# Wq's first half loaded in two pieces: 16 rows, then 112 rows

## The chip, the cores and the metric

The kernel runs on one core of a Trainium2 chip. The metric is device time in microseconds (us), lower is better; three runs of the kernel before gave 198.17, 198.26 and 198.59, with 198.26 as the median. All else comes from one profiled execution, which took 198.21.

## The reference

One decoding step of an attention layer with a gate beside it, for a batch of 8 tokens of width 512. All tensors are bf16.

```
xn = layernorm(x)                                    # 8 x 512
q  = xn @ wq                                         # wq 512 x 4096: 32 heads of 128
k, v = the last 2048 positions of the caches         # 8 batches x 8 kv heads x 2048 x 128 each
s  = softmax(q k^T * 128^-0.5) v @ wo                # 4 query heads share a kv head
g  = silu((sigmoid(xn @ w_gate) * (xn @ w_up)) @ w_down)   # inner width 1792
out = x + s * g
```

The work is small beside the data: the two cache windows are 32 MB each (33.6 million bytes), Wq and Wo 4 MB each, and the three weights of the gate 1.75 MB each.

## The kernel before

All large inputs are loaded by DMA on SP's queue, in tiles of 128 rows (partitions), through one pool of nine buffers (`RING`, the tag "ring"). A tile is 2 MB for Wq's halves, K, V and Wo's halves, and 1.75 MB for the gate's weights. In a K, V or Wq tile each partition holds one run of 16 KB. The function `load` (L88) issues a transfer on SP unless it is told otherwise.

The order of the loads is written out by hand (`loads`, L138 to L146): Wq's two halves, then K and V tiles in turn, where V tile i comes `PV_LAG` steps after K tile i, then the gate's weights and Wo in parts of falling size. A loop (`issue_loads`, L164) issues a load when its buffer has been released by the work on an earlier tile; the framework puts the semaphore waits before it. The completion semaphores of these loads are eight that are used in turn, so a load also waits for the one eight places before it on the hardware queues. The tiny x is loaded once on ACT's queue (`x_bf`, L97, 8 rows of 1 KB) and once on GpSimd's (L184).

Wq is 512 rows of 4096. Row 4p + kt lies on partition p (`wq_view`, L99), so that each partition has four rows of 8 KB; the first half (`wq_sb0`) takes rows kt = 0 and 1, the second kt = 2 and 3. Both stand in memory with a pitch of 32 KB from partition to partition. Their transfers (L104) are the first two that SP issues.

Then the layernorm runs on DVE and ACT (L200 to L228), and `q_projection` (L357) multiplies: 16 matmuls on the first half, 16 on the second (L367). `q_out` (L378) copies and turns q into the block layout `qz_sb` that the scores need. After it a loop of slots runs K's turns on DVE (`k_turn`, L422), the scores on TensorE (`qk`, L435), softmax (L447 to L512), and the product with V (`pv`, L549), each a few slots behind the one before. The gate's matmuls are near the end, and Wo's (L662) last, followed by two DVE instructions and the store of the result.

Of the kernel before, what the change touches and what calls it, by code (L numbers as in the profile page):

```python
# [10 lines left out]
def kernel(  # L11
# [14 lines left out]
    P = 128  # L26
# [32 lines left out]
    CB = CH // C4  # L59
    PV_WIDE = 6  # L60
    RING = 9
    NCOL = 2
    DC = D // NCOL

# [10 lines left out]
    small = ctx.enter_context(tc.tile_pool(name="small", bufs=2))  # L75
    ring = ctx.enter_context(tc.tile_pool(name="ring", bufs=RING))
    ppool = ctx.enter_context(tc.tile_pool(name="ppool", bufs=2))
# [10 lines left out]
    def load(dst, src, q=None):  # L88
        if q is None:
            q = nc.sync  # L90
        q.dma_start(out=dst, in_=src)

    def ring_tile(shape, name):
        return ring.tile(shape, bf16, name=name, tag="ring", align_bytes=ALIGN)
# [4 lines left out]
    wq_view = A_wq.rearrange("(p kt) n -> p kt n", kt=KT)  # L99
    KH = KT // 2  # L100
    wq_sb = []
    for kh in range(2):
        t = ring_tile([P, KH, Hq * Dh], f"wq_sb{kh}")
        load(t[:], wq_view[:, kh * KH : (kh + 1) * KH, :])  # L104
        wq_sb.append(t)

    k_tiles = {}
# [56 lines left out]
    def issue_loads():  # L164
        while loads_done[0] < len(loads):
            n = loads_done[0]
            if n >= RING and loads[n - RING] not in released:
                break
            kind, i = loads[n]
            if kind == 0:  # L170
                k_tiles[i] = load_kv(A_k_cache, i, "k_sb")
            elif kind == 1:
                v_tiles[i] = load_kv(A_v_cache, i, "v_sb")
            elif kind == 2:
                load_mlp(i)
            else:
                load_wo(i)
            loads_done[0] += 1

    issue_loads()  # L180
    x2_sb = work.tile([NCOL * 32, DC], bf16, name="x2_sb")
    nc.gpsimd.memset(x2_sb[:], 0.0)
    for j in range(NCOL):
        nc.gpsimd.dma_start(  # L184
# [124 lines left out]
    hT_sb = work.tile([P, FT, 32], bf16, name="hT_sb")  # L309
    gate = work.tile([NCOL * 32, DC], f32, name="gate")  # L310

# [26 lines left out]
    def unit_out():  # L338
        b_ps = psum1.tile([NCOL * 32, DC], f32, name="b_ps", tag="misc")
        for t in range(FT):  # L340
            for j in range(NCOL):
                nc.tensor.matmul(
                    b_ps[32 * j : 32 * (j + 1), :],
                    lhsT=hT_sb[:, t, :],
                    rhs=wd_sb[0][:, t, DC * j : DC * (j + 1)],
                    start=(t == 0),
                    stop=(t == FT - 1),
                    tile_position=(0, 32 * j),
                    skip_group_check=True,
                )  # L350
        sigb = work.tile([NCOL * 32, DC], f32, name="sigb")
        nc.scalar.activation(out=sigb[:], in_=b_ps[:], func=AF.Sigmoid)
        nc.vector.tensor_tensor(out=gate[:], in0=sigb[:], in1=b_ps[:], op=ALU.mult)
# [357 lines left out]
```

## Time and profile before

| what | value |
|---|---|
| median of three runs | 198.26 us |
| the profiled execution: its time, its span | 198.21 us, 196.5 us |
| DMA: moved, mean rate | 81.19 MB, 413 GB/s |
| SP's queue: packets, share of 16 engines' span | 6752, 97.1% |
| Wq's two issues on SP | 407 and 421 ns |
| Wq, from issue to landing | 7.6 and 11.8 us |
| first q matmul; first of the second half | 8.49 us; 13.16 us |
| last part of Wo landed | 192.96 us |

The span runs from the first to the last instruction of the program; the device's time includes 1.71 us around it. In the table of 40 slices a digit is the busy share of a slice in tenths. DMA stands for the mean of the core's 16 DMA engines. The chain of waits is followed back from the last instruction, at each step to what released it; a stretch of the chain that is called DMA runs from the issue of a transfer to its landing, so it contains the time in which it was queued behind others. Beside these views the trace has a record of every DMA packet: its start, its duration and its bytes. A row of 16 KB is one packet.

### The profile page before, as it was taken

How to read it: one execution, taken by the hardware profiler on the slowest of the kernel's cores; microseconds unless marked ns; L12 is line 12 of the kernel's file. 1: busy time of each engine (PE TensorE's matmuls, PEld its weight loads, DVE VectorE, ACT ScalarE, POOL GpSimd, SP SyncE). 2: the span in 40 equal slices, each digit the busy share in tenths (PEclk: the TensorE clock that was granted, in tenths of full speed). 3: DMA queues.
4: the chain of work that ended last, by engine and by line, in shares of the span. 5: the costliest groups of instructions: out<-in, count | busy, mean ns of one | idle time of the engine just before them, and what ended most of it. 6: DMA issues, size and time to landing. Idle time of an engine off the chain costs nothing.

```text
span 196.5 us, 2699 instructions
## 1 busy us (share of the span) xinstructions
PE 138.2 (70%) x1112; PEld 57.6 (29%) x1112; DVE 117.0 (60%) x200; ACT 32.6 (17%) x68; POOL 9.3 (5%) x21
## 2 busy tenths in 40 slices
PE   0340078669998987899789278946794779674783
PEld 0110011032324222423333044404240424443661
DVE  3818999746686828664777277837773750361101
ACT  3008540410121102101210021002100210340000
POOL 8820000000000000000000000000000000000000
PEclk9999999955999997879999957996888587996579
DMA  6999999999999999999999999999999999999991
GB/s 215 429 427 427 430 434 429 440 434 427 434 427 434 427 427 427 430 434 430 430 434 434 424 427 440 430 425 427 430 434 430 427 431 434 423 424 420 411 391 41
DMA packets 6860, 81.19 MB, mean 413 GB/s; under 512 B 792, under 2 KB 1088, under 8 KB 2112
## 3 DMA queue, kind: packets, MB, share of 16 engines
q1 hardware_dynamic: 6752, 81.01, 97.1%
q8 instruction: 8, 0.13, 0.2%
q10 hardware_dynamic: 32, 0.01, 0.1%
q14 instruction: 4, 0.03, 0.0%
q0 software_dynamic: 64, 0.01, 0.0%
HBM read 81.02 MB, written 0.01 MB: 412 GB/s over the span
## 4 chain that ended last, share of the span: by engine, by line
DMA 72%; DVE 17%; PE 8%; ACT 1%; issue 1%; SPq 0%; DVEq 0%; ACTq 0%
DMA k_sb<-in_A_k_cache_dram 47%; DMA wd_sb<-in_B_w_down_dram 14%; DVE k_sb L422 11%; DMA wq_sb<-in_A_wq_dram 6%; DMA wo_sb<-in_A_wo_dram 5%; PE pT_ps L486 3%; PE s_ps L435 3%; DVE qz_sb L395 2%; PE acc_ps L549 1%; DVE mx L447 1%; DVE qT_sb L386 1%; DVE pt_bf L475 1%; ACT L461 1%; PE q_ps L367 1%; PE mb_ps L456 0%
## 5 line engine op out<-in xcount | busy, mean ns | idle before, releaser
L422 DVE STREAM_TRANSPOSE k_sb<-k_sb 128x1024 f32<-128x1024 f32 x64 | 75.9, 1219 | 16.6 <-DMA k_sb<-in_A_k_cache_dram 16.5
L435 PE MATMUL s_ps<-k_sb,qz_sb 128*32 128x512 bf16 x256 | 68.7, 1065 | 16.4 <-DVE k_sb L422 11.6
L549 PE MATMUL acc_ps<-v_sb,pT_sb 128*32 128x256 bf16 (+1 forms) x416 | 35.3, 345 | 3.9 <-DMA v_sb<-in_A_v_cache_dram 2.6
L549 PEld LDWEIGHTS <-pT_sb 128*32 128x32 bf16 (+1 forms) x416 | 12.5, 109 | 33.2 <-issue 27.0
L506 DVE TENSOR_SCALAR pT_sb<-pc_bf,Hm 128x512 bf16<-128x512 bf16 x32 | 9.1, 349 | 18.3 <-ACT pc_bf L495 18.3
L435 PEld LDWEIGHTS <-qz_sb 128*32 128x32 bf16 x256 | 8.3, 100 | 34.0 <-issue 26.1
L560 ACT COPY acc_sb<-acc_ps 128x256 f32<-128x256 f32 (+1 forms) x16 | 7.2, 453 | 63.2 <-PE acc_ps L549 63.2
L486 PE MATMUL pT_ps<-pt_bf,spread 128*128 128x128 bf16 x128 | 12.5, 272 | 6.3 <-DVE pt_bf L475 6.3
L570 PEld LDWEIGHTS oT_ps<-Sel,acc_sb 128*128 128x128 f32 x88 | 11.8, 202 | 14.3 <-ACT acc_sb L560 8.5
L570 PE MATMUL oT_ps<-Sel,acc_sb 128*128 128x16 f32 x88 | 13.4, 276 | 1.1 <-ACT acc_sb L560 1.1
L486 PEld LDWEIGHTS <-spread 128*128 128x128 bf16 x128 | 10.8, 123 | 10.8 <-DVE pt_bf L475 10.8
L456 PE MATMUL mb_ps<-mj,SumM 128*128 128x4 f32 x16 | 3.5, 286 | 14.3 <-DVE mj L449 14.3
L461 ACT ACTIVATE p_bf<-s_ps,nm 128x512 bf16<-128x512 f32 x8 | 5.5, 687 | 46.5 <-DVE nm L458 46.5
L577 DVE TENSOR_TENSOR oT_sb<-oT_ps,rden 128x16 bf16<-128x16 f32 x16 | 2.6, 160 | 11.7 <-PE oT_ps L570 11.7
L456 PEld LDWEIGHTS mb_ps<-mj,SumM 128*128 128x128 f32 x16 | 2.8, 218 | 22.5 <-DVE mj L449 20.6
L397 ACT COPY qz_sb<-qT_sb 32x128 bf16<-32x128 bf16 x20 | 8.3, 413 | 3.0 <-DVE qT_sb L386 2.7
L530 DVE RECIPROCAL rden<-den_ps 128x32 f32<-128x32 f32 x8 | 2.8, 351 | 7.3 <-PE den_ps L528 7.3
L495 ACT CAST pc_bf<-pT_ps 128x512 bf16<-128x512 f32 x8 | 4.7, 587 | 13.1 <-PE pT_ps L486 13.1
L367 PE MATMUL q_ps<-wq_sb,xnT_sb 128*32 128x512 bf16 x32 | 3.8, 625 | 4.0 <-DMA wq_sb<-in_A_wq_dram 4.0
L475 DVE STREAM_TRANSPOSE pt_bf<-p_bf 128x512 bf16<-128x512 bf16 x8 | 5.4, 679 | 1.9 <-ACT p_bf L461 1.9
L662 PE MATMUL a_ps<-wo_sb,o_sb 128*32 128x256 bf16 x64 | 5.5, 315 | 1.0 <-DMA wo_sb<-in_A_wo_dram 0.9
L447 DVE TENSOR_REDUCE mx<-s_ps 128x1 f32<-128x512 f32 x8 | 5.3, 657 | 0.0
(61 smaller groups left out, 61.9 us busy)
## 6 DMA issues: line engine op xcount, KB each, us to landing
k_sb<-in_A_k_cache_dram SPq DMA_DIRECT2D x16, 2048.0 KB, 31.8
v_sb<-in_A_v_cache_dram SPq DMA_DIRECT2D x16, 2048.0 KB, 29.5
wq_sb<-in_A_wq_dram SPq DMA_DIRECT2D x2, 2048.0 KB, 9.7
wo_sb<-in_A_wo_dram SPq DMA_DIRECT2D x2, 1024.0 KB
wg_sb<-in_B_w_gate_dram SPq DMA_DIRECT2D x1, 1792.0 KB, 29.3
wu_sb<-in_B_w_up_dram SPq DMA_DIRECT2D x1, 1792.0 KB, 30.1
wd_sb<-in_B_w_down_dram SPq DMA_DIRECT2D x1, 1792.0 KB, 27.6
wo_sb<-in_A_wo_dram SPq DMA_DIRECT2D x3, 512.0 KB, 23.5
```

Of the source, the lines that this page charges most:

```text
L397: nc.scalar.copy(out=out, in_=in_)
L422: nc.vector.transpose(out=kw, in_=kw)
L435: nc.tensor.matmul(s_tiles[b][32 * gl : 32 * (gl + 1), :], lhsT=qz_sb[:, b, GL * gg + gl, j, :], rhs=kT[:, :, a, :, gl, e], start=(gg == 0 ...
L447: nc.vector.reduce_max(out=mx[:], in_=s_tiles[b][:], axis=AX.X)
L456: nc.tensor.matmul(mb_ps[:], lhsT=SumM[:], rhs=mj[:], start=True, stop=True)
L461: nc.scalar.activation(out=p_bf[:], in_=s_tiles.pop(b)[:], func=AF.Exp, bias=nm[:], scale=scale, accum_out=den128[:],)
L475: nc.vector.transpose(out=pt_bf[:].rearrange("p c g q r -> p (c g q r)"), in_=p_bf[:])
L486: nc.tensor.matmul(pT_ps[:, :, c4, :], lhsT=spread[:, c4, Q, :], rhs=pt[:, :, Q, :], start=(Q == 0), stop=(Q == NQ - 1), skip_group_check= ...
L506: nc.vector.tensor_scalar(out=pT_tiles[b][:, :, gl, :], in0=pc, scalar1=Hm[:, gl : gl + 1], scalar2=None, op0=ALU.mult,)
L549: nc.tensor.matmul(acc_tiles[i][w * c : w * (c + 1), :], lhsT=pT[:, 32 * y : 32 * y + w], rhs=v_tiles[i][:, ch : ch + n_ch, :].rearrange(" ...
L560: nc.scalar.copy(out=acc_sb[:], in_=acc_tiles.pop(i)[:])
L570: nc.tensor.matmul(oT_ps[:], lhsT=acc_sb[:, Dh * c : Dh * (c + 1)], rhs=sel[:, c // 2, c % 2], start=(c == 0), stop=(c == n_ch - 1),)
```

## The change

The first half of Wq is no longer loaded by one transfer of 128 rows. Two transfers fill the same tile: the first brings partitions 0 to 15, one run of 16 KB for each of the 16 DMA engines, and the second partitions 16 to 127. The second half stays one transfer, and so do all other loads. SP issues one DMA more (47 in place of 46); no other engine's instructions change, apart from the semaphores on which they wait.

```diff
     RING = 9
+    HEAD = 16
...
     for kh in range(2):
         t = ring_tile([P, KH, Hq * Dh], f"wq_sb{kh}")
-        load(t[:], wq_view[:, kh * KH : (kh + 1) * KH, :])
+        rows = (0, HEAD, P) if kh == 0 else (0, P)
+        for r0, r1 in zip(rows, rows[1:]):
+            load(t[r0:r1], wq_view[r0:r1, kh * KH : (kh + 1) * KH, :])
         wq_sb.append(t)
```

## The prediction

> **What bounds the kernel now.** I read the page's first two parts first: is any engine full, or are the transfers?
>
> ```profile
> span 196.5 us, 2699 instructions
> ...
> PE 138.2 (70%) x1112; PEld 57.6 (29%) x1112; DVE 117.0 (60%) x200; ACT 32.6 (17%) x68; POOL 9.3 (5%) x21
> ...
> DMA  6999999999999999999999999999999999999991
> ```
>
> No compute engine is above 70%, while the DMA row stands at 9 in every slice but the first and the last. So the end of the kernel is the start of the transfers, plus 81 MB at a fixed pace, plus a short tail. The chain of waits at both ends says the same: Wq's transfers hold the first 13 us, and from 155 us the chain goes through the loads of w_down and Wo to four short instructions.
>
> ```profile
> 1.29 11.84 DMA wq_sb<-in_A_wq_dram
> 13.16 1.07 PE q_ps L367 x8
> ...
> 155.44 27.61 DMA wd_sb<-in_B_w_down_dram
> ...
> 183.06 9.89 DMA wo_sb<-in_A_wo_dram
> ```
>
> Between these the chain runs for a while through DVE (k_sb, L422), but the DMA engines never run dry: loads are issued about 30 us before they land (DMA issues: k_sb 31.8, v_sb 29.5), about six 2 MB tiles ahead. If Wq comes later, q, the K turns, the released buffers and the next issues all come later by the same amount, and the queue keeps its depth. So a delay or gain in the first transfer reaches the end one for one. The table of stretches shows the start up close (us, then busy times, and last the clock, the DMA share and GB/s):
>
> ```profile
> 0.00:1.75 1.75, 0.00 (x0) 0.00 (x0) 0.00 (x0) 0.31 (x1) 0.85 (x6) 1.00 0.00 0
> 1.75:2.25 0.50, 0.00 (x0) 0.00 (x0) 0.00 (x0) 0.50 (x1) 0.50 (x2) 1.00 1.75 344
> 2.25:3.25 1.00, 0.00 (x0) 0.00 (x0) 0.60 (x2) 0.47 (x1) 0.93 (x4) 1.00 0.57 180
> 3.25:8.25 5.00, 0.29 (x4) 0.31 (x5) 4.22 (x11) 0.29 (x1) 4.74 (x5) 1.00 0.99 418
> ...
> 43.25:183.25 140.00, 111.75 (x918) 46.19 (x919) 83.93 (x144) 18.53 (x39) 0.00 (x0) 0.85 1.01 429
> ```
>
> Nothing moves before 1.75 us, the pace is poor until 3.25, and then it is within 3% of the 429 GB/s of the middle. In the trace's records of single packets (start and duration of each) the poor stretch is this: each of the 16 DMA engines begins its first 16 KB row of Wq between 1.855 and 2.755 us (mean 2.20), that row takes 632 to 1438 ns (mean 1128), and all 16 first rows end between 2.99 and 3.50 (mean 3.32). From then on a row takes 611 ns, on every engine, nearly back to back. That is the whole room for a gain: an unhindered row would save at most 1128 - 611 = 0.52 us, and a start of all engines at the first one's 1.855 another 0.34.
>
> **The change, part by part.**
>
> *One more issue on SP.* The two Wq issues take 407 and 421 ns, so every later one of the first burst moves by 0.41 us: the first K load's issue goes from 1.74 to 2.15, and its bytes are wanted only after Wq, at about 13. Covered by 10 us: 0. Without that cover it would cost 0.41.
>
> *Waits that move.* The loads use eight completion semaphores in turn, so each load waits for the eighth before it. With one more in the row, the sixth K or V load, issued at 5.20 us behind x's long landed semaphore, will wait for the 16-row piece (here at about 4.5), and the next for the 112 rows as it did for the first half; further ones keep their old partners. Queued behind it on SP are loads whose bytes are needed 30 us later: 0. PE's first q matmul (8.49) now waits for two transfers; behind it stand the 31 other q matmuls. The 112 rows are issued last and land last, so the wait for the 16 adds nothing, and PE idles 2.77 us before the second half anyway: 0.
>
> *Sixteen more completion packets* of 4 bytes, one for each engine, 9 ns and some 6 ns of gap: +0.015 us.
>
> *The start of the first rows.* The only small transfer on such a queue is x_bf (8 rows, L97): issued at 0.81 like Wq, its packets start between 1.779 and 1.853, where Wq's spread over 0.9 us. With 16 rows I expect the same close start, at about 1.83 for all engines, 0.37 before today's mean. The 112 rows, issued 0.42 later, are ready at about 2.6 (today's 2.20 and 0.42), before any first row is through.
>
> *The first rows themselves.* Today each engine's first row is one of the eight that it takes of 128, and after 3.5 us these run at 611 ns on all 16 engines at once, so there they do not hinder each other. The new head sends them to 16 neighbouring partitions. No transfer of before does that at this size. From below: the unhindered 611 ns. From above: all 16 in turn, 16 x 0.611 = 9.8 us. The nearest row is again x_bf, 8 neighbouring partitions: its eight packets take 51, 44, 293, 44, 461, 260, 44 and 44 ns, 1241 together, 3.5 times eight unhindered ones. Some of that may be the first read's latency, which the Wq rows have too. I take 3.5 x 0.611 = 2.15 us, and the 0.52 us of first latency ahead of it as today: 1.83 + 0.52 + 2.15 = 4.50, against 3.32. **Term: +1.2 us**; ends -0.9 (0.52 + 0.37) and +8.9 (1.83 + 0.52 + 9.8 - 3.32).
>
> Here the Trainium skill has a price: SBUF — State Buffer, section "Door 1: The DMA port swizzle (why [64,N] ≈ [32,N])", says that partitions 0 to 15 reach 4 of 16 ports and measured 104 GB/s. By it the 256 KB would take 2.5 us in place of my 2.15, and the term would be +1.6. No run shown here moves such a piece.
>
> *The other 112 rows.* Spread over the 16 engines as evenly as the 128 are now (eight packets each), they are 7 per engine, so the borders between engines no longer fall where those of 128 rows do, and two engines come to write into one neighbourhood at once for part of the time. From below: 0, the 611 ns of the 128-row transfers, which are the nearest in size; from above, 3.5-fold on all 7 rows as in x_bf, 7 x 2.5 x 0.611 = +10.7. But a stretch of eight neighbours, which in x_bf has eight engines in it, has only two at 7 rows each: two by turns throughout would cost 7 x 0.611 = 4.3. I take half the time shared: **+2.1 us**. The engines run their own lists without waiting for each other, and the end is set by the last one, so I do not lower this for those that meet nobody.
>
> **The sum**, on the profiled execution: its span is 196.5 and its time 198.21, 0.05 below the median of 198.26. 198.21 + 1.2 + 2.1 + 0.015 = **201.5 us**, 1.6% slower.
>
> **Rivals.**
>
> 1. *Only the 16 rows are hindered*; the 112 are laid out as harmlessly as 128. For it: every 128-row transfer runs at 611 ns. Time 198.21 + 1.2 = **199.4**. Chance 0.18.
>
> 2. *The 112 rows go out by turns*, one row to each engine, so that all 16 engines stand on neighbours seven more times. Against it: the 128-row transfer shows no trace of such turns. 198.21 + 1.2 + 10.7 = **210.1**. Chance 0.06.
>
> 3. *Faster: neighbours do not hinder each other*, and only the earlier start is left. Place: the first row of each engine; price: 0.37 us of earlier start plus up to 0.52 of first latency, less the 0.015. It decides if a 16 KB row into neighbouring partitions takes less than about 1.4 us (3.32 - 1.83 = 1.49, less some margin). For it: x_bf's five packets of 44 to 51 ns, which show no hindrance at all. Against it: its three long ones. Half of the 0.9 is what the 112 rows' readiness at about 2.6 to 3.2 leaves: **197.7**. Chance 0.10.
>
> 4. *The change does not do what it says*: first rows are late because memory answers late, whatever is asked, and 16 rows end at 3.3 as today. 198.2, and nothing would be seen. Chance 0.04. The rule that two transfers in place of one share the same 16 engines and bring nothing (DMA: Bandwidth & Descriptors, section "Rules for kernel authors", in the Trainium skill) ends here; the trace's full DMA row agrees, but only for times after 3.25 us.
>
> **How the numbers follow.** The forecast holds 0.62. Its own range is 200.3 to 202.9: the head from 0.7 (no first latency ahead of it) to 1.5 (four by turns, 4 x 0.611, in place of 3.5), the body from 1.4 to 3.2 (shared for a third to three quarters of the time). The range to give goes further down, to rival 1 with its head cut to 0.7: 198.9 to 202.9. It holds the forecast and rival 1, 0.80, and leaves out rivals 2, 3 and 4, 0.20. A measurement of this kernel can tell 0.2% (0.4 us) from no change. Slower: forecast, rivals 1 and 2, 0.86. Rival 3 gives 0.08 to faster and 0.02 to no change, and rival 4 adds its 0.04 there: 0.06.
>
> **What would show it.** Right: the GB/s of 2 to 4.5 us falls to about a third or a quarter of 429 rather than rising at 3.25; the first q matmul starts at about 11.8 in place of 8.49, and the second half's at 16.5 in place of 13.16; w_down and Wo land 3.3 us later, with DMA still at 9 in all slices between. Packets of 16 KB longer than 611 ns appear between 1.8 and 12 us and nowhere later. Rival 1: the long packets are the 16 first ones alone. Rival 2: the first half lands at about 20 us. Rival 3: first q matmul before 8.3. The prediction is wrong altogether if a DMA engine goes idle later, or if Wq is late and Wo's last landing (192.96) is not.

## The result, and the profile after

The changed kernel takes 201.69 us (median of five runs, 201.3 to 202.35) against 198.26 (median of five). The ratio is 1.0168, with a 95% interval of 1.0149 to 1.0187: about 1.7% slower, 3.4 us. The profiled execution is the slowest of the five, 202.35 us with a span of 200.6. (The profiled execution of one kernel below, the first with four added pieces, was a slow one, so that kernel was run a second time.)

The page of the changed kernel shows the same full DMA row, but its first three slices move fewer bytes. First the GB/s of the kernel before, then three lines of the changed one:

```profile
GB/s 215 429 427 427 430 434 429 440 434 427 434 427 434 427 427 427 430 434 430 430 434 434 424 427 440 430 425 427 430 434 430 427 431 434 423 424 420 411 391 41
```

```profile
span 200.6 us, 2701 instructions
...
DMA  6999999999999999999999999999999999999990
GB/s 126 272 366 434 425 431 434 430 425 428 438 431 425 431 434 431 425 428 441 428 425 428 438 428 428 428 436 428 425 434 434 428 429 422 441 425 414 410 381 26
```

This is the point to see: "busy" stays at 9 while the rate is 272 and 366 in place of the 429 and 427 of before. An engine that is held up counts as busy. The bytes show it, the share does not. The table of stretches puts the loss between 3.25 and 13.25 us (the last two columns are the DMA share and GB/s; in the kernel before, 2.25 to 3.25 us was already poor, at 180):

```profile
1.75:2.25 0.50, 0.00 (x0) 0.00 (x0) 0.00 (x0) 0.50 (x1) 0.50 (x2) 1.00 1.65 340
2.25:3.25 1.00, 0.00 (x0) 0.00 (x0) 0.00 (x0) 0.47 (x1) 0.93 (x4) 1.00 1.27 199
3.25:4.50 1.25, 0.00 (x0) 0.00 (x0) 1.12 (x1) 0.00 (x0) 1.25 (x1) 1.00 0.82 131
4.50:8.25 3.75, 0.00 (x0) 0.00 (x0) 3.38 (x4) 0.27 (x1) 3.48 (x6) 1.00 0.99 276
8.25:13.25 5.00, 0.93 (x12) 0.55 (x16) 3.59 (x14) 0.03 (x1) 1.93 (x6) 1.00 0.97 296
13.25:43.25 30.00, 14.22 (x74) 2.68 (x66) 22.98 (x34) 11.41 (x25) 0.00 (x0) 1.00 1.01 431
```

In the kernel before, the last two of these stretches were:

```profile
8.25:13.25 5.00, 1.99 (x20) 0.74 (x23) 2.36 (x7) 0.00 (x0) 2.34 (x7) 1.00 1.03 442
13.25:43.25 30.00, 15.81 (x82) 3.85 (x81) 24.23 (x37) 12.08 (x26) 0.00 (x0) 0.92 1.01 431
```

From 13.25 us on the rate is the same, 431 GB/s. The chain at both ends agrees:

```profile
1.71 15.27 DMA wq_sb<-in_A_wq_dram
...
17.02 1.07 PE q_ps L370 x8
...
159.04 27.88 DMA wd_sb<-in_B_w_down_dram
...
186.94 9.92 DMA wo_sb<-in_A_wo_dram
```

Wq's second half lands at 16.98 in place of 13.12 (+3.86), Wo's last part at 196.86 in place of 192.96 (+3.90), and the chain's last load takes as long as before (9.92 and 9.89 us).

The records of single packets give the cleanest measure. Take the 16 KB packets of the loads in order of their start, 16 at a time, as many as there are engines, and compare the mean start of the n-th group in the two kernels:

```
group (16 packets)         1      2      3      5      9     10     13     41    101    261
start, after - before  -0.05  +0.07  +1.11  +1.92  +3.24  +3.66  +3.70  +3.70  +3.70  +3.70 us
```

The whole loss is made in nine groups and stays at 3.70 us to the end. This "shift of the stream" is used for the experiments below, beside the ratio of times. It belongs to one execution of each kernel, here to the slowest of five, whose spans go from 199.4 to 200.6 us.

One caution on these records: a packet's record ends before its bytes are in place. The records of the 16 rows in the changed kernel end at 3.37 us on average, but the signals of their completion, one from each engine, come at 4.93 on average (4.33 to 5.66). In the kernel before, the eighth row's records end at 7.69 and the signals come at 8.23. A hold-up therefore shows in part in the packet behind: the 16 rows themselves are recorded with 1.23 us on average (before: 1.12), the first of the 112 rows with 1.74.

### The profile page after: what moved, and what is told of

Same layout as the page of the kernel before. It is cut to its first block, busy times and chain, and to the rows that moved or that the text cites. A ratio compares the mean times of both kernels' runs of the same rounds, so it can differ in the third digit from the quotient of the medians.

```text
span 200.6 us, 2701 instructions
## 1 busy us (share of the span) xinstructions
PE 138.2 (69%) x1112; PEld 56.6 (28%) x1112; DVE 117.8 (59%) x200; ACT 32.5 (16%) x68; POOL 8.9 (4%) x21
## 4 chain that ended last, share of the span: by engine, by line
DMA 72%; DVE 16%; PE 8%; ACT 1%; issue 1%; SPq 0%; DVEq 0%; ACTq 0%
DMA k_sb<-in_A_k_cache_dram 46%; DMA wd_sb<-in_B_w_down_dram 14%; DVE k_sb L425 11%; DMA wq_sb<-in_A_wq_dram 8%; DMA wo_sb<-in_A_wo_dram 5%; PE s_ps L438 3%; PE pT_ps L489 2%; DVE qz_sb L398 2%; PE acc_ps L552 1%; DVE mx L450 1%; DVE pt_bf L478 1%; DVE qT_sb L389 1%; ACT L464 1%; PE mb_ps L459 1%; PE q_ps L370 1%
## 5 line engine op out<-in xcount | busy, mean ns | idle before, releaser
L665 PE MATMUL a_ps<-wo_sb,o_sb 128*32 128x256 bf16 x64 | 4.8, 275 | 1.7 <-DMA wo_sb<-in_A_wo_dram 1.6
```

## The experiments

The theory: a DMA engine that writes into a partition takes turns with the others that write nearby. In a 128-row transfer no two engines meet; in one of 16 neighbouring rows about four do at each place, and in one of 112 rows two do for part of the time. Its rivals: the extra transfer as such costs, or a small first transfer spoils the start, or only one of the two pieces is dear. All ratios are to the kernel before on the same chip, with 95% intervals. A diff that removes a line `rows = ...` is against the changed kernel, the others are against the kernel before.

**Only the place of the split** (Wq's second half, when the engines are already running):

```diff
-        rows = (0, HEAD, P) if kh == 0 else (0, P)
+        rows = (0, HEAD, P) if kh == 1 else (0, P)
```

> The same split, 16 rows and 112 rows, made in Wq's second half instead of the first, so that the engines are already running when the pieces come. Theory of turns: the loss of 3.4 us does not hang on the start, 201.2 to 202.2. Rival, the loss is one of the start (a short first transfer, late first rows): 198.3.

Measured: ratio 1.0222 (1.0202 to 1.0243), +4.4 us; the stream shifts by 3.73 us, as in the changed kernel. In this run the poor stretch is the one from 8 us on:

```profile
3.25:8.25 5.00, 0.29 (x4) 0.31 (x5) 4.19 (x12) 0.29 (x1) 4.79 (x5) 1.00 1.10 405
8.25:13.25 5.00, 1.90 (x16) 0.49 (x15) 2.56 (x8) 0.00 (x0) 2.49 (x8) 1.00 0.94 233
13.25:17.25 4.00, 0.08 (x4) 0.08 (x8) 0.00 (x0) 0.00 (x0) 0.00 (x0) 1.00 0.97 299
```

So the loss does not hang on the start. The time, 202.76 us, is a little above the range given, and 0.7 us of it lie beyond the stream's shift. In the profiled execution the last DVE instruction starts 3.85 us later than before (197.61 against 193.76), so most of the 0.7 lies behind that instruction; its cause is open.

**Two pieces along the columns** instead of the rows, 128 partitions in both:

```diff
-        load(t[:], wq_view[:, kh * KH : (kh + 1) * KH, :])
+        for c in range(KH):
+            if kh == 0:
+                load(t[:, c : c + 1], wq_view[:, c : c + 1, :])
+        if kh == 1:
+            load(t[:], wq_view[:, KH:, :])
```

> Wq's first half in two transfers again, but split along the columns of the tile: all 128 partitions in both, 8 KB for each. One more transfer and a smaller first one as in the change, without any change of which engine writes where. Theory of turns: no loss, 198.0 to 198.5, and at best the 0.2 us by which a smaller first transfer starts earlier. Rival, the extra transfer or the wait for two of them is what costs: about 201.7.

Measured: ratio 1.0005 (0.9989 to 1.0020), no difference. **Then with a narrow first piece**, 2 KB on each partition, as many bytes as the 16 rows:

```diff
-        load(t[:], wq_view[:, kh * KH : (kh + 1) * KH, :])
+        cols = (0, 1024, KH * Hq * Dh) if kh == 0 else (0, KH * Hq * Dh)
+        flat = wq_view[:, kh * KH : (kh + 1) * KH, :].rearrange("p k n -> p (k n)")
+        for c0, c1 in zip(cols, cols[1:]):
+            load(t[:].rearrange("p k n -> p (k n)")[:, c0:c1], flat[:, c0:c1])
```

> Wq's first half in two transfers along the columns again, the first of 2 KB for each of the 128 partitions (256 KB, as many bytes as the 16 rows), the second of 14 KB. A small first piece that reaches every partition. Theory of turns: nothing lost, at best the start's 0.2 us gained, 198.0 to 198.4. Rival, a small first piece costs as such: about 201.7.

Measured: ratio 1.0017 (1.0001 to 1.0034), +0.3 us by the median, slightly above the range. An extra transfer, an extra wait and a small first piece cost 0 to 0.3 us; the rival that makes them the cause falls. They bring nothing either: the room at the start, up to 0.86 us by the prediction's count, was reached by neither.

**Nothing but 16-row pieces:**

```diff
-        rows = (0, HEAD, P) if kh == 0 else (0, P)
+        rows = range(0, P + 1, HEAD) if kh == 0 else (0, P)
```

> Wq's first half is loaded by eight transfers of 16 neighbouring rows instead of one of 128. Theory of turns (engines that write to neighbouring partitions wait for each other, about four to a turn): each 16-row piece takes 4 x 0.611 = 2.4 us instead of 0.61, so 198.3 + 8 x 1.83 = about 212.9, and every one of the eight rows per engine is slow in the packet records. Rival, a fixed price of the extra transfer (3.4 us for one more): 7 x 3.4, about 222. Rival, only the odd split of 112 rows is dear and the 16-row piece is free: about 198.5. Rival, only the very start is disturbed: 201.7 or less.

Measured: ratio 1.0608 (1.0579 to 1.0637), +12.0 us; the stream shifts by 11.57. Two stretches of it:

```profile
3.25:8.25 5.00, 0.00 (x0) 0.00 (x0) 4.63 (x4) 0.26 (x1) 4.72 (x6) 1.00 1.17 139
8.25:13.25 5.00, 0.29 (x4) 0.21 (x4) 3.58 (x14) 0.03 (x1) 1.94 (x7) 1.00 0.87 105
```

A third to a quarter of the rate, and the hold-up comes with each of the eight pieces: from the third row on a packet takes 2.138 us (median; 2.112 to 2.155), not quite the 2.44 expected, so the time is 210.28 us and not 212.9. The first row is recorded with 1.33 us and the row behind the eighth with 1.51 (medians); then come 611 ns. So the 16-row piece does cost, and a fixed price of 3.4 us for each extra transfer (222 us) is ruled out once more.

**Two pieces of 64 rows:**

```diff
+        rows = (0, 64, P) if kh == 0 else (0, P)
```

> Wq's first half in two transfers of 64 rows (partitions 0 to 63, then 64 to 127), nothing odd in the split: 4 rows for each engine in each. Theory of turns with partners 32 partitions apart: every row is shared by two, 1.28 us instead of 0.611 as measured on every eighth partition, 8 x 0.67 = +5.3, about 203.5. If only close neighbours hinder each other (groups of four belong to one engine here): 198.3. If an extra transfer as such costs: 201.7.

Measured: ratio 1.0269 (1.0243 to 1.0295), +5.3 us, stream +5.11. Half the rate throughout Wq's first half:

```profile
3.25:8.25 5.00, 0.29 (x4) 0.21 (x4) 4.22 (x11) 0.29 (x1) 4.72 (x7) 1.00 1.04 220
8.25:13.25 5.00, 0.00 (x0) 0.00 (x0) 2.37 (x8) 0.00 (x0) 2.36 (x7) 1.00 0.96 211
```

**The same 16 source rows to other partitions.** Four transfers of 16 rows are added between Wq and the first K load, into buffers of the ring that are not yet in use; nothing reads them. Only the destination differs between three kernels: `t[0:HEAD]` as below, `t[0:P:8]` or `t[0:32:2]`.

```diff
+    spares = [ring_tile([P, KH, Hq * Dh], f"spare{i}") for i in range(4)]
...
+    for t in spares:
+        load(t[0:HEAD], wq_view[0:HEAD, 0:KH, :])
```

> The kernel before, with four added transfers of 16 rows x 16 KB (partitions 0 to 15) between Wq and the first K load, into buffers of the ring that are not yet in use; nothing reads them. The bytes alone cost 4 x 0.611 = 2.4 us: 200.7 if 16 neighbouring rows run unhindered. Theory of turns by four: 4 x 2.44 = 9.8, about 208.0.

> As the run with four added 16-row transfers, the same source rows, but they land on every eighth partition (0, 8, ... 120). If the destination makes the turns, the engines meet less: two in one place instead of four would give 4 x 1.22 = 4.9 us, about 203.1, and none would give 200.7. Rival, the source rows or the small transfer as such are slow: the same as with neighbouring partitions.

> Four added 16-row transfers on every second partition (0, 2, ... 30), the same source rows as in the two runs before with neighbours and with every eighth. If partitions share a way in by groups of four, two engines meet at each: as with every eighth partition, about 203.7. If the groups are eight wide, four meet: as with neighbours, about 208.3. If a narrow stretch as such is slow: above 206.

> The kernel with four added 16-row transfers on partitions 0 to 15 once more, for an undisturbed profile: its times were 10.1 us above the kernel before, where four rows of 2.14 us, as measured when Wq came in eight such pieces, make 8.6. If the rows alone make it, 206.7; if something else is slow as well, 208.3, and the stream of packets should show where.

Measured: on partitions 0 to 15, ratio 1.0512 (1.0490 to 1.0534) (+10.1 us), and the second time 1.0492 (1.0462 to 1.0523), +9.8 us; on every eighth 1.0285 (1.0254 to 1.0315), +5.6; on every second of the first 32, 1.0273 (1.0245 to 1.0302), +5.4. The stretch in which the added rows come, in this order (neighbours the second time, every eighth, every second):

```profile
13.25:17.25 4.00, 1.90 (x16) 0.51 (x15) 1.21 (x3) 1.10 (x3) 0.00 (x0) 1.00 1.15 123
```

```profile
13.25:17.25 4.00, 1.90 (x16) 0.50 (x15) 1.73 (x5) 1.63 (x4) 0.00 (x0) 1.00 1.01 209
```

```profile
13.25:17.25 4.00, 1.90 (x16) 0.49 (x15) 1.51 (x4) 1.41 (x3) 0.00 (x0) 1.00 1.05 217
```

Behind the first of the four rows a packet takes 2.407 us (median) on neighbours, and 1.28 on every eighth as on every second partition, against 0.611: close to four, two and two by turns. The source, the number of bytes and the shape of the transfer are the same, so the destination decides. The stream of the second run with neighbours shifts by 9.84, which is four rows of 2.46, and the shift is the same from the 41st group of packets to the 200th, so the buffers that the added rows take from the ring hold nothing up; the 1.5 us that seemed too much had come from taking 2.14 for a row, and the first expectation, 4 x 2.44, was right.

That every eighth partition still makes two meet rules out that only close neighbours count. The Trainium skill (SBUF — State Buffer, section "Door 1: The DMA port swizzle (why [64,N] ≈ [32,N])") has the map: four neighbouring partitions share one of 16 ports, and the ones 32 further belong to the same port. By it 0 to 15 reach 4 ports, every eighth or every second as above 8, and 64 rows 8. All four runs agree: half the rate with 64 rows and on every eighth or second partition, a quarter on neighbours. The Trainium skill's limit there of about 109 GB/s for 0 to 15 is met by 16 packets of 16,384 bytes in 2.407 us, 109 GB/s.

**The 112 rows.** Two of them added in the same way, and one alone in place of Wq's first half:

```diff
+    spares = [ring_tile([P, KH, Hq * Dh], f"spare{i}") for i in range(2)]
...
+    for t in spares:
+        load(t[HEAD:P], wq_view[HEAD:P, 0:KH, :])
```

> The kernel before, with two added transfers of 112 rows x 16 KB (partitions 16 to 127) between Wq and the first K load, into ring buffers not yet in use; nothing reads them. The bytes cost 2 x 7 x 0.611 = 8.6 us: 206.7 if 112 rows run unhindered as 128 do. Theory as predicted, the 112 rows are hindered for half of the time: 2 x 2.1 more, 211. If all of the loss in the changed kernel is the 16-row piece: 206.7.

```diff
-        load(t[:], wq_view[:, kh * KH : (kh + 1) * KH, :])
+        r0 = HEAD if kh == 0 else 0
+        if kh == 0:
+            nc.vector.memset(t[:HEAD].rearrange("p k n -> p (k n)").bitcast(f32), 0.0)
+        load(t[r0:], wq_view[r0:, kh * KH : (kh + 1) * KH, :])
```

> Wq's first half by one transfer of the 112 rows only; partitions 0 to 15 of the tile are set to zero by DVE and these 64 rows of Wq are left out of the product. One row less for each engine is 0.61 us less. If the 112 rows are hindered as in the run with two added ones (5.35 / 2 = 2.7 us each): 198.2 - 0.6 + 2.7 = 200.3. If the 16-row piece makes the whole loss: 197.6.

(The tile of Wq's first half holds two rows of Wq on each partition, so 32 rows are left out, not 64.) Measured: two added, ratio 1.0694 (1.0658 to 1.0729), +13.8 us, stream +13.90, of which 14 rows of 0.611 are 8.55; 5.35 remain, 2.7 for each (2.1 expected). Alone: ratio 1.0090 (1.0059 to 1.0121), +1.8 us for one row less per engine; the stream shifts by 1.62, and with the missing row's 0.61 the hindrance is 2.23. Its stretch:

```profile
3.25:8.25 5.00, 0.00 (x0) 0.00 (x0) 4.53 (x7) 0.29 (x1) 5.00 (x2) 1.00 1.03 276
```

So the 112-row piece costs by itself, at the start and in the running stream, and in the stream it is the dearer of the two (2.7 against 1.85, which is 2.46 less 0.61).

**The other order**, 112 rows first:

```diff
-        rows = (0, HEAD, P) if kh == 0 else (0, P)
-        for r0, r1 in zip(rows, rows[1:]):
+        rows = ((HEAD, P), (0, HEAD)) if kh == 0 else ((0, P),)
+        for r0, r1 in rows:
             load(t[r0:r1], wq_view[r0:r1, kh * KH : (kh + 1) * KH, :])
```

> The changed kernel with the two pieces in the other order, 112 rows first, then 16. If the loss is the sum of what the two pieces do to their own rows: 201.5 to 202.5. If it is the small first piece that spoils the start: 198.3.

Measured: ratio 1.0213 (1.0184 to 1.0242), +4.2 us; stream +3.66. The shift is that of the changed kernel, so a small first piece is not what costs. The median time, 202.64 us, is just above the range and 0.9 us above the changed kernel's (the two intervals just touch); the stream does not show this difference.

## Why the prediction was right, point by point

- *The bound.* Right. The DMA stream is the bound, and a delay in Wq reaches the end of the stream one for one: +3.70 us at group 13 and +3.70 at group 261.
- *The extra issue, the moved waits, the completion packets.* Right at nothing to be seen. Two transfers along the columns have all three, and their ratio is 1.0005. The load that had to wait for the 16 rows did so until 5.67 us (their last signal of completion comes at 5.66, not at 4.5), which cost nothing that the stream shows.
- *The start.* Wrong by its gain. 0.37 us of earlier first rows was taken into the first term; they start at 2.14 us on average, against 2.19. With eight 16-row pieces it was 1.98.
- *The first rows.* The mechanism was right: a 16 KB row goes by turns, 2.41 us in the running stream where 2.15 were taken. That the factor 3.5 came so near four is luck. x_bf's eight packets, 3.5 times too long in sum before, take 708, 688, 79 and five times 44 ns in the changed kernel, and 399 and seven times 44 with eight 16-row pieces: waits of single packets, not turns of all. The term itself, +1.2 us, was a little high all the same, as the sum below shows. (Its upper end should read +8.8: 1.83 + 0.52 + 9.8 - 3.32.) The row time of 2.5 us that stood beside the sum as an estimate from the Trainium skill (SBUF — State Buffer, section "Door 1: The DMA port swizzle (why [64,N] ≈ [32,N])") was nearer to the 2.41, but its term of +1.6 was further off.
- *The 112 rows.* Right that they cost, low in size: 2.1 expected, 2.2 measured alone at the start and 2.7 for each in the running stream. The 2.1 was half of a bound of 4.3, a choice and not a measurement, and the reason given for it, two engines in one neighbourhood, is argued and not shown.
- *The sum.* Expected +3.3, measured 3.4 in the median and 3.70 in the profiled stream. The completions of the two pieces divide the 3.70 (us from issue to the last of them):

```profile
wq_sb<-in_A_wq_dram SPq DMA_DIRECT2D x1, 1792.0 KB, 11.2
...
wq_sb<-in_A_wq_dram SPq DMA_DIRECT2D x1, 256.0 KB, 4.9
```

  On average over the engines the 16 rows are complete at 4.93 us and the 112 at 11.95. Seven rows of 0.611 would take 4.28 of the 7.02 between, so by this division the 112 rows cost 2.7, and some 1.0 is left for the 16. The first term was 0.2 too high and the second 0.6 too low, and that the sum came so near is in part luck. The 16 rows cost 1.85 in the running stream and only 1.0 here; the first latency of 0.5, which the prediction put ahead of the turns in full, may cover some of them, but no run separates the two.
- *The signs to look for.* From 3.25 to 4.5 us the rate was 131 GB/s, as forecast; from 2.25 to 3.25 it did not fall (199, before 180). Packets of the loads longer than 0.65 us start between 1.8 and 11.82 us; later there are nine single ones, and nine in the kernel before too. Wo's last part lands 3.9 us later, forecast 3.3. The two halves of the q matmuls start later than forecast, 12.61 and 17.02 in place of 11.8 and 16.5. For the first, the engines also end further apart: the completions of the 112 rows come from 11.21 to 12.48 us, those of the first half before from 8.05 to 8.45, and the matmul waits for the last.
- *The rivals.* "Only the 16 rows" falls by the run of the 112 alone; "by turns on all 112" (210) by the time itself; "neighbours do not hinder" by the added rows; "nothing would be seen" (198.2) by the time too. The Trainium skill's rule that two transfers to halves of the partitions merely share the same engines and so bring nothing (DMA: Bandwidth & Descriptors, section "Rules for kernel authors") is too mild here: two pieces of 64 rows lost 5.3 us.

What stays open: how the 112 rows are dealt out to the engines. The records do not name the engine or the partition of a packet. That only some engines carry them does not fit the DMA share of 0.99 from 4.5 to 8.25 us. If each engine had 7 rows in a line and a port of its own for part of them, some packets should run at 611 ns; but between 4.5 and 11 us the packets of the changed kernel take 1.006 us in the median and none is below 0.733. That two engines meet at the borders is therefore argued, from the runs with 16 and 64 rows, and for this piece no run changes the destination alone; shown is that a 112-row transfer costs 2.2 to 2.7 us more than its bytes.

## What to carry to other kernels

Where the DMA stream is the bound, look at bytes per time and at the duration of single packets, because the busy share does not tell an engine at work from one that waits its turn. Split a load along the columns, with all 128 partitions in each piece, and not along the partitions: the first cost 0 to 0.3 us here, the second 3.4 to 12 us for 2 MB. A transfer to a few partitions is paid by all transfers behind it on the same engines.

## What the runs showed of the hardware that was not expected

Sixteen neighbouring rows took 2.407 us per packet when four such transfers went to the same partitions one after the other, and only 2.138 when eight of them went from one set of 16 to the next (123 GB/s in all); that neighbouring transfers overlap there is a guess. And a late x moves more than itself. In the changed kernel the cast of x starts, when x has landed, at 3.38 us in place of 2.61, after GpSimd's fill of qz_sb has begun (3.10 us, 3.51 long), and it lasts eight times as long (timeline of DVE, changed kernel, then before):

```profile
3.38 3.64 DVE L203 CAST x_f<-x_bf 8x512 f32<-8x512 bf16 x1 [3.38 <-DMA x_bf<-in_A_x_dram]
```

```profile
2.61 0.46 DVE L200 CAST x_f<-x_bf 8x512 f32<-8x512 bf16 x1 [2.61 <-DMA x_bf<-in_A_x_dram]
...
4.55 2.40 DVE L213 TENSOR_SCALAR xn_bf<-x_f,mv,rstd 8x512 bf16<-8x512 f32 x1
```

The columns are start, length, engine and operation. In the kernel before another instruction of DVE, L213, is the long one beside the same fill (0.53 us in the changed kernel, after the fill). It holds nothing up in either kernel, because the part of Wq that the first q matmul needs lands later still (12.48 us; the transposed x is ready at 9.58).
